# The first pair of a fused attention and cosine-gated MLP: order of gate and conversion, weight sums on VectorE, two homes for temporaries, exponentials in two steps

## Chip, cores and metric

The kernel runs on one core of one Trainium2 chip. The metric is the device time of one execution in microseconds (us). All arithmetic is in 32-bit floats; the two weight matrices arrive as 64-bit floats.

## What is computed

```python
# x: (8, 8, 512, 64)   state: (8, 8, 32, 64)   w_in: (512, 2048)   w_out: (2048, 512)
scores = scale * x @ state.T;  a  = softmax(scores);   xread = a @ state      # per batch and head
scores2 = scale * state @ x.T; a2 = softmax(scores2);  sread = a2 @ x
y = concatenate([xread, sread], axis=2)          # (8, 8, 544, 64)
y = y.transpose(0, 2, 1, 3).reshape(8 * 544, 512)
h = y @ w_in
g = h * cos(h)
out = g @ w_out
```

## The kernel before

**Tiles and steps.** The work goes by batches (eight), two of which make a pair, and in each batch by 16 tiles of 128 rows of `h`. One tile is one step, so the first pair is steps 0 to 31. For a tile PE (TensorE) makes 128 x 512 of `h` in PSUM (`hidden`, L490), and the gate follows in four instructions: ScalarE rounds `h` to an integer (`gate`, L560), VectorE (DVE) subtracts (`gate2`, L563), ScalarE takes the sine (`gate3`, L566), DVE multiplies (`gate4`, L580) and so puts `g` into `g_all`. In steps 0 to 27 (`first_pair`) a tile has one of two PSUM buffers, which the product frees.

**The order is written out by hand.** The program has no scheduler: the order of the instructions in the source is the order on each engine, and each engine runs its own in order. `plan(b)` lists for each step what else is done for attention: on PE, on ScalarE (`x_act`, `y_act`, `z_act`) and on DVE (`x_dve`, between the gate's subtraction and product; `y_dve`, behind the product). Its parts are the token turns (L310), the scores (L328), `max1`, `shift` and `exp1` for the first softmax, `max2` and `exp2` for the second, `sums`, `inverse`, `spread1`, `norm1`. Exponential and sine lie in different activation tables, so that a change from one to the other brings an ACT_TABLE_LOAD.

**Conversion.** The weights come in 18 loads of up to 1 MB of raw 64-bit numbers into three buffers (quads 9 to 11 of `g_all`; a quad is four slots of 128 x 512). `conv_at` gives a step to each of loads 4 to 17: in that step ScalarE makes two passes over it (L243, L246), in the next step DVE two (L249, L252) and Pool (GpSimd) the last addition (L257). As soon as DVE has read a raw buffer, SP issues the next load (`fetch`, L212). SP also issues, in its own order, token loads and x_b loads (L131), stores of weight blocks (L673), loads of weight blocks into a ring of four (L683), and the output's stores (L622).

**Two forms of the second product.** In steps 4 to 27 PE multiplies two quarters of `w_out` directly (`first_product`, `second_product`, L633). From step 29 on it works by the seven-product scheme of Strassen and Winograd on two levels: seven products with combinations of the quarters A11, A12, A21, A22, and each of these again in seven stages (L745) with combinations of its own four blocks. Pool forms the sums of `g` that the stages need (L692), and sums of the weights of the hidden tiles (`sw_sums`, L523).

**The weights of the seven-product scheme** are prepared once, in steps 16 to 25 (A12's in step 50). `weight_sum` combines whole quarters in place (`SQ` = A21 + A22, A21' = A11 - A21, A22' = SQ - A11, SQ' = A12 - A22'; L1092). `inner_weights(which, m)` makes, for one matrix, four temporaries t1 to t4 of 128 x 512 on Pool (L671) in one fixed quad (`TEMPS`, quad 4), and has SP store eight blocks in device memory (`blocks_kept`): four of the matrix, four temporaries. The next `inner_weights` writes the same quad, so it waits until the stores have read it. `weights_at[step]` holds these calls; they come behind the tile's own code in a step. Before the change, in this order: 16 A22; 17 SQ on Pool; 18 SQ, and A21' on DVE; 19 A11; 20 A22' on Pool; 21 A21'; 22 A22'; 24 SQ' on DVE; 25 SQ'. "Last set" below is that of SQ'.

**Order of a conversion step**, cut to what the change moves:

```python
gate(t); gate2(t)
go(1); go(3)                 # x_act, x_dve
convert(last, "bcdf")        # L249, L252 on DVE, L257 on Pool, next raw load
if conv >= 0 and not todo[1]: convert(conv, "1")
gate3(t)
gate4(t)
```

Of the kernel before, what the change touches and what calls it, by code (L numbers as in the profile page):

```python
# [13 lines left out]
ALU = mybir.AluOpType  # L14
# [8 lines left out]
def kernel(  # L23
# [8 lines left out]
    nc = tc.nc  # L32
# [43 lines left out]
    def quad(n):  # L76
        return g_all[:, QT * n:QT * n + QT]
# [186 lines left out]
    class Attention:  # L264
# [115 lines left out]
            self.exp2()  # L380

        def inverse(self, v):
            w = v.rearrange("p (a b) -> p b a", b=2)
            nc.vector.tensor_scalar(w, w, 1e-9, None, op0=ALU.add)
            nc.vector.reciprocal(v, v)
# [273 lines left out]
        m = m.rearrange("p (k i) (m d) -> p m k i d", k=2, m=2)  # L659
        return m[:, 0, 0], m[:, 0, 1], m[:, 1, 0], m[:, 1, 1]  # L660

    def inner_weights(which, m, temps=TEMPS):

        m11, m12, m21, m22 = quarters(m)
        t1, t2, t3, t4 = [quad(temps)[:, n].rearrange("p (i d) -> p i d", d=P)
                          for n in range(4)]
        for o, x1, x2, op in ((t1, m21, m22, ALU.add),
                              (t2, t1, m11, ALU.subtract),
                              (t3, m11, m21, ALU.subtract),
                              (t4, m12, t2, ALU.subtract)):  # L670
            nc.gpsimd.tensor_tensor(o, x1, x2, op=op)  # L671
        for n, block in enumerate((m11, m12, t4, m22, t1, t2, t3, m21)):
            nc.sync.dma_start(  # L673
                out=blocks_kept[which, n].rearrange("p (i d) -> p i d", d=P),
                in_=block)

    stage_list = []

# [279 lines left out]
    def plan(b):  # L958
        pe, x_act, y_act, x_dve, y_dve, z_act = [
            {s: [] for s in range(NF)} for _ in range(6)]  # L960

        def prod(s, b, nt, *bank):
            pe[s].append((b, "products", nt) + bank)
            x_act[s].append((b, "products_kept", nt) + bank)

        def pairs(s, b, name, kept, i):
            pe[s] += [(b, name, i), (b, name, i + 1)]
            x_act[s].append((b, kept, i))
            y_act[s].append((b, kept, i + 1))

        def early(b, s):
            if b == 1:
                pairs(s[0], b, "tokens", "tokens_kept", 0)
                pairs(s[1], b, "tokens", "tokens_kept", 2)
            else:
                for k in range(NK):
                    to = (x_dve, y_dve)[k % 2]
                    to[s[k // 2]].append((b, "tokens_turned", k))
            pe[s[2]].append((b, "scores"))
            x_dve[s[2]].append((b, "max1"))  # L980
            x_dve[s[3]].append((b, "spread1"))
            y_dve[s[3]].append((b, "shift"))
            if b == 1:
                x_dve[s[4]].append((b, "max2"))
                y_act[s[4]].append((b, "exps"))
            else:
                y_dve[s[4] - 1].append((b, "max2"))
                z_act[s[4]].append((b, "exps"))
            if b == 1:
                x_dve[s[5]].append((b, "sums"))  # L990
                y_dve[s[5]].append((b, "spread1"))
                x_dve[s[6]].append((b, "norm1"))
            else:
                y_dve[s[4]].append((b, "sums1"))
                x_dve[s[5]].append((b, "spread2"))
                y_dve[s[5]].append((b, "norm1"))

        def late(b, s):
            pairs(s[0], b, "turn", "turn_kept", 0)
            pe[s[1]].append((b, "reads", 0))  # L1000
            pe[s[2]].append((b, "reads", 1))
            x_dve[s[2]].append((b, "keep"))
            if len(s) > 3:
                turned(b, s[3])

        def turned(b, s):
            pe[s].append((b, "keep2"))
            x_act[s].append((b, "keep3"))


        if b == 0:
            pe[0].append((0, "products", 0, SIDE, HC, WC))
            y_dve[0] += [(0, "products_taken", 0, SIDE, HC, WC),
                         (0, "inverse2")]
            prod(7, 0, 2, SIDE)
            prod(11, 0, 3)
            prod(13, 1, 0, SIDE)
            late(0, (1, 2, 3, 4))
            early(1, (5, 6, 7, 8, 9, 10, 11))
            late(1, (12, 13, 14))  # L1020
        else:
            bank = (SIDE,) if b == 1 else ()
            if b == 1:
                turned(1, 0)
            prod(0, b, 1, *bank)
            prod(3, b, 2, *bank)
            prod(8, b, 3, *bank)
            if b + 1 < B:
                prod(12, b + 1, 0)
                early(b + 1, (1 + (b == 1), 2 + (b == 1), 4, 5, 7, 8, 9))  # L1030
                late(b + 1, (9, 10, 11, 15))
        return pe, x_act, y_act, x_dve, y_dve, z_act
# [37 lines left out]
    for n in range(B // 2):  # L1070
        end = n == B // 2 - 1
        for r, engine, o, x1, x2, half in (
                ((25, 26), dve, 0, 2, 0, 0), ((27, 28), dve, 0, 2, 0, 1),
                ((31, 31), pool, 2, 3, 2, 0), ((33, 33), dve, 0, 3, 0, 0),
                ((34, 34 + (not end)), dve, 0, 3, 0, 1),
                ((35, 36), dve, 2, 3, 2, 1),
                ((38 - end,) * 2, pool, 1, 1, 0, 0),
                ((39 - end,) * 2, pool, 1, 1, 0, 1)):
            for i in range(2):
                outer_at[PERIOD * n + r[i]].append(  # L1080
                    (engine, n, o, x1, x2, half, i))
# [3 lines left out]
                     for r in (o, x1, x2)]  # L1085
        sub(engine, o, x1, x2)

    def weight_sum(engine, o, x1, x2, op):
        n = 1 if engine is pool else 2
        for i in range(0, QT, n):  # L1090
            o_, x1_, x2_ = [quad(q)[:, i:i + n] for q in (o, x1, x2)]
            engine.tensor_tensor(o_, x1_, x2_, op=op)  # L1092

    def last_weights():
        temps = quads_free.pop(0)
        inner_weights(1, a12, temps)
        weights_at[53].append(lambda: quads_free.extend([A12, temps]))

    A11, A12, A21, A22, SQ = 5, 6, 7, 8, 11
    add_, sub_ = ALU.add, ALU.subtract  # L1100
    for at_, what in (
            (15, lambda: quads_free.append(10)),
            (16, lambda: inner_weights(2, a22)),
            (17, lambda: quads_free.append(9)),
            (17, lambda: weight_sum(pool, SQ, A21, A22, add_)),
            (18, lambda: inner_weights(3, matrix(SQ))),
            (18, lambda: weight_sum(dve, A21, A11, A21, sub_)),
            (19, lambda: inner_weights(0, a11)),
            (20, lambda: weight_sum(pool, A22, SQ, A11, sub_)),
            (21, lambda: inner_weights(5, matrix(A21))),  # L1110
            (22, lambda: inner_weights(4, matrix(A22))),
            (23, lambda: quads_free.append(A11)),
            (24, lambda: weight_sum(dve, SQ, A12, A22, sub_)),
            (25, lambda: quads_free.append(A21)),
            (25, lambda: inner_weights(6, matrix(SQ))),
            (27, lambda: quads_free.extend([A22, SQ, TEMPS])),
            (50, last_weights)):
        weights_at[at_].append(what)

# [19 lines left out]
    def first_pair(step, t):  # L1139
        last, conv = conv_at.get(step - 1, -1), conv_at.get(step, -1)  # L1140
        if step == 4:
            warm(1, acc[0])
        if step != 1:
            hidden(t)
        if step == 0:
            hidden(all_tiles[1])
            warm(3, acc[0])
            gate(t)
            gate2(t)
            convert(3, "bcdf")  # L1150
            convert(4, "1")
            go(0)
        else:
            go(0)
            if step == 5:
                states(1, side_banks[0])
            gate(t)
            gate2(t)
            if step == 3:
                warm(4, acc[0])  # L1160
                part(0, "products", 1, SIDE)
            go(1)
            go(3)
            if step == 1:
                convert(4, "bcdf")
            elif last >= 0:
                convert(last, "bcdf")
            if conv >= 0 and not todo[1]:
                convert(conv, "1")
        gate3(t)  # L1170
        go(5)
        if step == 3:
            part(0, "products_kept", 1, SIDE)
        gate4(t)
        if conv >= 0 and todo[1] and step > 0:
            convert(conv, "1")
        if step == 6:
            states_kept(1, side_banks[0])
        go(2)
        if conv >= 0:  # L1180
            convert(conv, "2")
        go(4)
# [124 lines left out]
```

## Time and profile before

| | us |
|---|---|
| median of 4 runs | 765.42 (764.69 to 765.94) |
| profiled execution | 765.93 |
| its span, first to last instruction | 764.1 |
| busy in the span: PE / DVE / ScalarE / Pool | 720.5 / 490.4 / 330.9 / 517.5 |

The profile comes from one execution. Its page gives busy time by engine, the span in 40 equal slices (each digit the busy share in tenths), and the chain of work that ended last: a walk back from the last instruction, at each step to what released it. Asked for a stretch, the trace gives that chain in order of time (start, length, what), or a timeline by engine: start, length, engine, line, operation, operands, count, and in brackets the engine's idle time just before and what ended it. A name like L692 is a line of the kernel before. In the kernel after the change the same code stands one to some thirty lines further down. SPq is SP's queue of DMA issues. PEclk, the clock granted to PE, was 0.991 of full speed over the span.

### The profile page before, as it was taken

Reading aid. Unit: us, or ns where it says so; the run is one execution under the profiler, and the core shown is the slowest. Engines: PE = TensorE matmul, PEld = TensorE weight load, DVE = VectorE, ACT = ScalarE, POOL = GpSimd, SP = SyncE. Lnnn points to the kernel's source line nnn. Section 1 sums busy time; section 2 is a strip of 40 time slices with the busy share of each in tenths; the row PEclk is TensorE's granted clock in tenths of the full one; section 3 lists DMA queues with packets and bytes.
Section 4 is the critical chain, followed back from the end, with each engine's and each line's share of the span. In section 5 each row is a group of like instructions: output and inputs, shape, how many; then the busy total and the mean of one; then the engine's idle time right before and its main releaser. Section 6 shows DMA issues by size and latency. Waiting matters only on the chain.

```text
span 764.1 us, 10471 instructions
## 1 busy us (share of the span) xinstructions
PE 720.5 (94%) x3552; PEld 506.6 (66%) x3552; DVE 490.4 (64%) x683; ACT 330.9 (43%) x538; POOL 517.5 (68%) x480
## 2 busy tenths in 40 slices
PE   8988887779999999999999999999999999999998
PEld 3443322336777876677768876677778767888886
DVE  5768786783876656685966666759746446264650
ACT  3877962633454445434373445343634432211110
POOL 2344267779699895368998953489989534799600
PEclk9999998999999999999999999999999999999999
DMA  8495359779423685476225943682224556445661
GB/s 247 166 275 167 125 121 267 224 246 182 116 87 80 138 236 142 109 146 166 73 80 111 183 112 95 134 195 84 71 69 124 111 155 163 114 147 184 185 156 41
DMA packets 210356, 111.32 MB, mean 146 GB/s; under 512 B 158272, under 2 KB 173120, under 8 KB 210304
## 3 DMA queue, kind: packets, MB, share of 16 engines
q1 hardware_dynamic: 209216, 110.14, 55.5%
q8 instruction: 28, 0.46, 0.2%
q10 hardware_dynamic: 960, 0.39, 0.2%
q14 instruction: 24, 0.20, 0.1%
q0 software_dynamic: 128, 0.13, 0.1%
HBM read 87.03 MB, written 23.59 MB: 145 GB/s over the span
## 4 chain that ended last, share of the span: by engine, by line
PE 60%; POOL 20%; DVE 5%; DMA 4%; issue 4%; ACT 3%; SPq 3%; POOLq 0%; DVEq 0%; ACTq 0%
PE o L745 31%; POOL g_all L692 12%; PE h L490 10%; PE h L540 9%; POOL g_all L671 4%; PE at L328 3%; PE at L846 2%; POOL swS_all L523 2%; PE at L425 1%; DMA blocks_kept<-g_all 1%; DMA g_all<-blocks_kept 1%; DMA x_b<-in_x_dram 1%; POOL sw L523 1%; SPq L131 1%; SPq L673 1%
## 5 line engine op out<-in xcount | busy, mean ns | idle before, releaser
L692 POOL TENSOR_TENSOR g_all<-g_all 128x512 f32<-128x512 f32 x256 | 336.7, 1350 | 108.3 <-PE o L745 62.9
L745 PE MATMUL o<-g_all 128*128 128x256 f32 x1456 | 345.2, 382 | 4.8 <-POOL g_all L692 3.4
L745 PEld LDWEIGHTS o<-g_all 128*128 128x128 f32 x1456 | 273.9, 191 | 65.7 <-issue 18.0
L563 DVE TENSOR_TENSOR q_all<-q_all,h 128x1024 f32<-128x1024 int32 (+1 forms) x88 | 85.4, 970 | 59.6 <-ACT q_all L560 59.5
L490 PE MATMUL h<-aT,sw 128*128 128x512 f32 x224 | 109.0, 611 | 12.7 <-DVE g_all L580 12.0
L566 ACT ACTIVATE q_all<-q_all,halfpi 128x1024 f32<-128x1024 f32 (+1 forms) x88 | 84.2, 957 | 61.7 <-DVE q_all L563 61.6
L580 DVE TENSOR_TENSOR g_all<-h,q_all 128x1024 f32<-128x1024 f32 (+1 forms) x88 | 85.7, 974 | 34.5 <-ACT q_all L566 32.2
L560 ACT ACTIVATE q_all<-h 128x1024 int32<-128x1024 f32 (+1 forms) x88 | 73.3, 833 | 75.4 <-DVE g_all L580 32.3
L490 PEld LDWEIGHTS h<-aT,sw 128*128 128x128 f32 x224 | 41.7, 194 | 59.8 <-issue 32.2
L549 DVE TENSOR_TENSOR h<-h,sums_all 128x256 f32<-128x256 f32 x72 | 30.9, 429 | 63.7 <-PE h L540 49.0
L692 DVE TENSOR_TENSOR g_all<-g_all 128x1024 f32<-128x1024 f32 x40 | 56.9, 1437 | 0.1
L540 PE MATMUL h<-aS_all,swS_all 128*128 128x256 f32 x144 | 45.8, 400 | 7.5 <-POOL swS_all L523 5.7
L540 PE MATMUL h<-aT,sw 128*128 128x256 f32 x144 | 44.6, 392 | 3.0 <-DVE g_all L580 2.5
L750 ACT COPY o<-o 128x256 f32<-128x256 f32 x26 | 9.3, 357 | 88.1 <-PE o L745 88.1
L671 POOL TENSOR_TENSOR g_all<-g_all 128x512 f32<-128x512 f32 x28 | 37.8, 1370 | 12.5 <-DMA blocks_kept<-g_all 11.9
L257 POOL TENSOR_TENSOR w_in<-w_in,aS_all 128x1024 int32<-128x1024 int32 (+1 forms) x10 | 19.3, 1926 | 37.4 <-DVE w_in L252 20.3
L540 PE MATMUL h<-aS_all,sw 128*128 128x256 f32 x144 | 43.6, 384 | 0.0
L540 PEld LDWEIGHTS h<-aS_all,swS_all 128*128 128x128 f32 x144 | 25.5, 191 | 26.8 <-POOL g_all L692 7.5
L756 ACT COPY o<-sums_all 128x256 f32<-128x256 f32 x26 | 9.8, 377 | 74.0 <-PE o L745 74.0
L603 DVE SCALAR_TENSOR_TENSOR held<-o,held 128x512 f32<-128x512 f32 x40 | 27.1, 680 | 21.3 <-PE o L745 20.8
L461 ACT COPY sw<-at 128x512 f32<-128x512 f32 x50 | 26.8, 588 | 31.3 <-PE at L328 31.3
L257 POOL TENSOR_TENSOR g_all<-g_all,aS_all 128x1024 int32<-128x1024 int32 x8 | 18.9, 2368 | 29.9 <-DVE g_all L252 22.6
(112 smaller groups left out, 867.5 us busy)
## 6 DMA issues: line engine op xcount, KB each, us to landing
g_all<-blocks_kept SPq DMA_DIRECT2D x202, 256.0 KB, 2.8
blocks_kept<-g_all SPq DMA_DIRECT2D x56, 256.0 KB, 3.0
g_all<-in_moe_w_out_dram SPq DMA_DIRECT2D x8, 1024.0 KB, 5.0
out_dram<-ot SPq DMA_DIRECT2D x128, 64.0 KB, 2.0
g_all<-in_moe_w_in_dram SPq DMA_DIRECT2D x6, 1024.0 KB, 5.7
xT<-in_x_dram SPq DMA_DIRECT2D x96, 64.0 KB, 3.0
x_b<-in_x_dram SPq DMA_DIRECT2D x24, 256.0 KB, 4.9
x_b<-in_x_dram SPq DMA_DIRECT2D x16, 128.0 KB, 4.0
```

Of the source, the lines that this page charges most:

```text
L257: nc.gpsimd.tensor_tensor(bits, bits, e, op=ALU.add)
L490: nc.tensor.matmul(out=t.hp, lhsT=t.lhs(i), rhs=t.rhs(i), start=(i == 0), stop=(i == t.kn - 1))
L540: nc.tensor.matmul(out=out_, lhsT=w, rhs=r, start=start, stop=True, skip_group_check=True)
L549: nc.vector.tensor_tensor(o, h2[:, LO], sums_all[:, 0], op=ALU.add)
L560: nc.scalar.activation(t.q.bitcast(I32), t.hp, func=ACTF.Copy, bias=0.25)
L563: nc.vector.tensor_tensor(t.q, t.q.bitcast(I32), t.hp, op=ALU.subtract)
L566: nc.scalar.activation(t.q, t.q, func=ACTF.Sin, bias=halfpi, scale=-TWO_PI)
L580: nc.vector.tensor_tensor(g, t.hp, t.q, op=ALU.mult)
L603: nc.vector.scalar_tensor_tensor(out=out.t[:, ch], in0=bank, scalar=TWO_PI, in1=b.t[:, ch], op0=ALU.mult, op1=ALU.add)
L671: nc.gpsimd.tensor_tensor(o, x1, x2, op=op)
L692: engine.tensor_tensor(o[:, i:i + n], x1[:, i:i + n], x2[:, i:i + n], op=ALU.subtract)
L745: nc.tensor.matmul(out=o, lhsT=ring[(self.first + k) % NB][:, i], rhs=g[:, i], start=(start and i == 0), stop=(i == QT - 1), skip_group_ch ...
```

## The change

1. In the first pair's steps the gate's product goes ahead of DVE's and Pool's conversion of the last load. (Step 0 stays as it was.)
2. All four weight sums run on DVE, each in two pieces of 128 x 1024, a piece a step: SQ in 16 and 17, A21' in 18 and 19, A22' in 20 and 22, SQ' in 23 and 25. None is left on Pool.
3. Pool's temporaries have two homes: quad 4 and `aS_all`, which conversion uses until step 16 and the hidden tiles from step 28. They take turns. A11's set comes first, one temporary in each of steps 12 to 15, and Pool's instructions are 128 x 256 in place of 128 x 512. The sets come in steps 12 to 15, 17, 19, 21, 23, 26.
4. The stores of a set are handed to SP at the start of the following step.
5. For batch 2 the second softmax's maximum and the first's exponential are in step 22, its sums and the second exponential in step 23, the inverse and `spread1` in step 24, `norm1` in step 25; before, the two exponentials were together in step 23. ScalarE's first copy of the turned second softmax follows the sine of its step.
6. One DVE sum of `g` (L692) moves from step 25 to 24.

```diff
-    def inner_weights(which, m, temps=TEMPS):
+    def inner_weights(which, m, temps, pieces=range(4), n=2):
...
-            nc.gpsimd.tensor_tensor(o, x1, x2, op=op)
-        for n, block in enumerate((m11, m12, t4, m22, t1, t2, t3, m21)):
-            nc.sync.dma_start(
...
+            for j in range(0, QT, n):
+                nc.gpsimd.tensor_tensor(o[:, j:j + n], x1[:, j:j + n],
+                                        x2[:, j:j + n], op=op)
+
+        def send():
+            for n, block in enumerate((m11, m12, t4, m22, t1, t2, t3, m21)):
+                nc.sync.dma_start(
...
+        if 3 in pieces:
+            stores_due.append(send)
...
+            elif b == 2:
+                x_dve[s[4] - 1].append((b, "max2"))
+                z_act[s[4] - 1].append((b, "exp1"))
+                x_dve[s[4]].append((b, "sums1"))
+                z_act[s[4]].append((b, "exp2"))
+                x_dve[s[5]].append((b, "inverse", None))
+                y_dve[s[5]].append((b, "spread1"))
+                x_dve[s[5] + 1].append((b, "norm1"))
...
+            if b == 2:
+                x_act[s[0]].remove((b, "turn_kept", 0))
+                y_act[s[0]].insert(0, (b, "turn_kept", 0))
...
-                ((25, 26), dve, 0, 2, 0, 0), ((27, 28), dve, 0, 2, 0, 1),
+                ((25 - (not n), 26), dve, 0, 2, 0, 0),
+                ((27, 28), dve, 0, 2, 0, 1), ((31, 31), pool, 2, 3, 2, 0), ((33, 33), dve, 0, 3, 0, 0),
...
+    def weight_sum(o, x1, x2, op, i):
+        o_, x1_, x2_ = [quad(q)[:, 2 * i:2 * i + 2] for q in (o, x1, x2)]
+        nc.vector.tensor_tensor(o_, x1_, x2_, op=op)
...
+    temps = [quad(TEMPS), aS_all.rearrange("p n i s -> p (n i s)").rearrange(
+        "p (t s) -> p t s", s=S)]
+    for i in range(QT):
+        weights_at[12 + i].append(lambda i=i: inner_weights(
+            0, a11, temps[0], (i,)))
+    for steps, o, x1, x2, op in (
+            ((16, 17), SQ, A21, A22, ALU.add),
+            ((18, 19), A21, A11, A21, ALU.subtract),
+            ((20, 22), A22, SQ, A11, ALU.subtract),
+            ((23, 25), SQ, A12, A22, ALU.subtract)):
+        for i in range(2):
+            weights_at[steps[i]].append(
+                lambda o=o, x1=x1, x2=x2, op=op, i=i: weight_sum(
+                    o, x1, x2, op, i))
     for at_, what in (
             (15, lambda: quads_free.append(10)),
-            (16, lambda: inner_weights(2, a22)),
             (17, lambda: quads_free.append(9)),
-            (17, lambda: weight_sum(pool, SQ, A21, A22, add_)),
-            (18, lambda: inner_weights(3, matrix(SQ))),
-            (18, lambda: weight_sum(dve, A21, A11, A21, sub_)),
-            (19, lambda: inner_weights(0, a11)),
-            (20, lambda: weight_sum(pool, A22, SQ, A11, sub_)),
-            (21, lambda: inner_weights(5, matrix(A21))),
-            (22, lambda: inner_weights(4, matrix(A22))),
+            (17, lambda: inner_weights(2, a22, temps[0])),
+            (19, lambda: inner_weights(3, matrix(SQ), temps[1])),
+            (21, lambda: inner_weights(5, matrix(A21), temps[0])),
+            (23, lambda: inner_weights(4, matrix(A22), temps[1])),
             (23, lambda: quads_free.append(A11)),
-            (24, lambda: weight_sum(dve, SQ, A12, A22, sub_)),
             (25, lambda: quads_free.append(A21)),
-            (25, lambda: inner_weights(6, matrix(SQ))),
-            (27, lambda: quads_free.extend([A22, SQ, TEMPS])),
+            (26, lambda: inner_weights(6, matrix(SQ), temps[0])),
+            (27, lambda: quads_free.append(A22)),
+            (28, lambda: quads_free.extend([SQ, TEMPS])),
...
             go(1)
             go(3)
-            if step == 1:
-                convert(4, "bcdf")
-            elif last >= 0:
-                convert(last, "bcdf")
             if conv >= 0 and not todo[1]:
                 convert(conv, "1")
         gate3(t)
...
         gate4(t)
+        if last >= 0:
+            convert(last, "bcdf")
```

More of the change, by code (lines that the diff above doesn't have):

```diff
@@ L382, in inverse @@
         def inverse(self, v):
+            v = self.i12 if v is None else v
             w = v.rearrange("p (a b) -> p b a", b=2)
@@ L660, in quarters @@
         return m[:, 0, 0], m[:, 0, 1], m[:, 1, 0], m[:, 1, 1]
-    def inner_weights(which, m, temps=TEMPS):
+    def inner_weights(which, m, temps, pieces=range(4), n=2):
         m11, m12, m21, m22 = quarters(m)
-        t1, t2, t3, t4 = [quad(temps)[:, n].rearrange("p (i d) -> p i d", d=P)
+        t1, t2, t3, t4 = [temps[:, n].rearrange("p (i d) -> p i d", d=P)
                           for n in range(4)]
[L667 to L671, printed above, removed]
-        for n, block in enumerate((m11, m12, t4, m22, t1, t2, t3, m21)):
-            nc.sync.dma_start(
-                out=blocks_kept[which, n].rearrange("p (i d) -> p i d", d=P),
-                in_=block)
+        for i in pieces:
+            o, x1, x2, op = ((t1, m21, m22, ALU.add),
+                             (t2, t1, m11, ALU.subtract),
+                             (t3, m11, m21, ALU.subtract),
+                             (t4, m12, t2, ALU.subtract))[i]
+            for j in range(0, QT, n):
[4 more added lines that the diff above has]
+                nc.sync.dma_start(
+                    out=blocks_kept[which, n].rearrange("p (i d) -> p i d",
+                                                        d=P),
+                    in_=block)
+        if 3 in pieces:
+            stores_due.append(send)
     stage_list = []
@@ L992, in early @@
                 x_dve[s[6]].append((b, "norm1"))
-            else:
+            elif b > 2:
                 y_dve[s[4]].append((b, "sums1"))
@@ L1072 @@
         for r, engine, o, x1, x2, half in (
-                ((25, 26), dve, 0, 2, 0, 0), ((27, 28), dve, 0, 2, 0, 1),
-                ((31, 31), pool, 2, 3, 2, 0), ((33, 33), dve, 0, 3, 0, 0),
+                ((25 - (not n), 26), dve, 0, 2, 0, 0),
+                ((27, 28), dve, 0, 2, 0, 1), ((31, 31), pool, 2, 3, 2, 0), ((33, 33), dve, 0, 3, 0, 0),
                 ((34, 34 + (not end)), dve, 0, 3, 0, 1),
@@ L1086, in outer_sum @@
         sub(engine, o, x1, x2)
[L1088 to L1092, printed above, removed]
+    def weight_sum(o, x1, x2, op, i):
+        o_, x1_, x2_ = [quad(q)[:, 2 * i:2 * i + 2] for q in (o, x1, x2)]
+        nc.vector.tensor_tensor(o_, x1_, x2_, op=op)
     def last_weights():
         temps = quads_free.pop(0)
-        inner_weights(1, a12, temps)
+        inner_weights(1, a12, quad(temps), n=QT)
@@ L1097, in last_weights @@
         weights_at[53].append(lambda: quads_free.extend([A12, temps]))
     A11, A12, A21, A22, SQ = 5, 6, 7, 8, 11
-    add_, sub_ = ALU.add, ALU.subtract
+    temps = [quad(TEMPS), aS_all.rearrange("p n i s -> p (n i s)").rearrange(
[12 more added lines that the diff above has]
+                    o, x1, x2, op, i))
```

## Prediction, made before the result

> **What bounds the kernel now.** I read the page's slices first, then the chain that ended last, in order of time, then the timelines of VectorE (DVE), ScalarE and GpSimd (Pool) where that chain leaves TensorE.
>
> ```profile
> PE   8988887779999999999999999999999999999998
> POOL 2344267779699895368998953489989534799600
> ```
>
> A slice is 19.1 us. PE has holes only in the first nine, which is the first pair (to about 172 us). After that PE is the bound, apart from three Pool stretches that come once in each later pair and that the change doesn't touch. So the change can win or lose only ahead of the point where PE is full, and later work moves with that point. The chain there, in order of time:
>
> ```profile
> 107.00 2.36 POOL g_all L257
> ...
> 114.41 3.81 POOL g_all L1092 x4
> 118.22 2.10 issue
> 120.35 2.31 POOL g_all L671
> 122.74 3.73 POOL g_all L671 x3
> ...
> 127.94 2.72 DMA blocks_kept<-g_all
> ...
> 137.47 2.82 DMA blocks_kept<-g_all
> ...
> 156.58 2.74 DMA blocks_kept<-g_all
> ...
> 181.61 3.06 DMA g_all<-blocks_kept
> ```
>
> From the last conversion (L257) to 165 us the chain is Pool: weight sums (L1092), temporaries (L671), and between two sets of temporaries the wait until the last set is stored. From there SP issues without a hole until the block that PE takes at 184.8. The timelines show the two costs:
>
> ```profile
> 116.88 2.27 DVE L1092 TENSOR_TENSOR g_all<-g_all 128x1024 f32<-128x1024 f32 x1 [3.88 <-POOL g_all L1092]
> 120.30 1.22 DVE L1092 TENSOR_TENSOR g_all<-g_all 128x1024 f32<-128x1024 f32 x1 [1.16 <-POOL g_all L1092]
> 122.16 0.72 ACT L566 ACTIVATE q_all<-q_all,halfpi 128x512 f32<-128x512 f32 x1 [8.39 <-DVE q_all L563]
> 130.74 5.09 POOL L671 TENSOR_TENSOR g_all<-g_all 128x512 f32<-128x512 f32 x4 [4.28 <-DMA blocks_kept<-g_all]
> 159.45 5.76 POOL L671 TENSOR_TENSOR g_all<-g_all 128x512 f32<-128x512 f32 x4 [3.83 <-DMA blocks_kept<-g_all]
> 108.83 0.69 DVE L580 TENSOR_TENSOR g_all<-h,q_all 128x512 f32<-128x512 f32 x1 [0.79 <-ACT q_all L566]
> 139.08 1.06 ACT L366 ACTIVATE aT<-aT 128x1024 f32<-128x1024 f32 x1
> ```
>
> DVE's sum of step 18 waits for Pool's sum of step 17, and the gates behind it wait with it: no sine for 8.39 us. Pool waits about four microseconds for stores (4.28, 3.77, 3.83). The 0.79 is what DVE idles when nothing stands between the gate's subtraction (L563) and its product (L580).
>
> **The sum, by step.** I follow the start of L563 of each step, before against after, and then Pool's last set of temporaries, which ended at 165.21.
>
> *Gate product ahead of conversion, steps 1 to 9 and 12 to 16.* The conversion's L249 and L252 (0.69 and 1.23) stood in the shadow of the sine; now DVE idles 0.79 first, and L252 ends 0.79 + 0.68 = 1.5 later in its step. It costs nothing where the next step's L563 waited longer than 0.79 for ScalarE anyway (after steps 1, 4 and 5: 1.44, 1.08 and 3.54 us). It costs in three places:
> - Steps 2 to 6. SP issues the next raw load only behind L252, and such a load lands 5.0 to 5.7 us later (median rows). In step 2 the delay is 1.5; in step 3 the load that was issued at 32.58 comes 1.5 later, ScalarE's first conversion (it waited 0.2 for it already) holds up the sine, and L252 ends 2.5 later. Queued behind it on SP are the eight x_b loads at 42.06 which PE waited for (6.18 us in the chain). So step 6 starts at 57.7, not 55.28.
> - Step 6. The states' copy (L171) now stands behind L249 and L252: another 0.9 for the scores of batch 1 that PE makes from it. Step 9 starts at 74.3, not 70.82: 3.5 late. Steps 9 to 13 keep that.
> - Steps 14 and 15. The last two raw loads are issued behind L252 of steps 12 and 13; the last one made ScalarE wait 0.74 before. With 1.5 more, the first conversion, which in these two steps stands ahead of the sine, holds up the gate by about 0.8 each. Step 16 starts at 108.05, not 103.06: 5.0 late.
>
> From below this is 0 (all of it covered by ScalarE, which is nearly full there); from above 14 x 0.79 = 11.1 if DVE ends last in every conversion step.
>
> *Temporaries of A11 in steps 12 to 15.* Eight Pool instructions of 256 elements. There is no such row; 128 elements take 0.46 (L523) and 512 take 1.27 (L671), so between 0.64 (half) and 1.27, and I take 0.73 on the line between them. They stand in Pool's holes of 1.95 to 2.94 us between conversions: nothing, and if that cover is gone 1.5 a step.
>
> *Weight sums on DVE.* Eight of 1.22 (L1092 undisturbed; 2.27 is the disturbed one). The first, in step 16, adds 1.2: step 17 starts at 113.6, not 107.37, 6.2 late. Then each step is the sum of its DVE issues (0.60 for L563 and L580 each when followed closely, 0.6 to 0.7 for a token turn, 1.2 for maximum, spread or shift, 0.79 or 0.17 idle) and 1.15 for the sum, with 0.4 for disturbance by Pool (it was 1.05 and 0.0 in the two L1092 rows above, with Pool pieces of 1.27; I take 0.5 of the one and scale it to 0.73 pieces, rounded up): step 17 takes 3.6 (it waits for Pool's last conversion), 18 to 20 4.3 each, 21 3.8: 20.3. Before, these steps took 133.08 - 107.37 = 25.7, since the wait for Pool was in them. Step 22 starts at 133.9, not 133.08: 0.8 late.
>
> The Trainium skill, "SBUF — State Buffer", section "Who interferes with whom", speaks against this part: a DVE instruction with two SBUF inputs and a GpSimd instruction that reads SBUF lock each other out for a whole instruction. By that rule each of the five sums ahead of step 22 could wait one full piece, and my estimate of the Pool piece would make it 1.7 us more than I take. The 2.27 row agrees; the 1.22 row, beside a Pool set that took 6.11 instead of 5.10, shows that the wait can also fall on Pool.
>
> *Exponentials in two steps (22 and 23).* Two more table loads, 1.28 each by the ACT_TABLE_LOAD rows. ScalarE after the sine of step 22: load, exp1 1.06, gate copy 0.6, load, sine 0.72, load, two exponentials 1.4, gate copy, two copies 1.06, load, sine: the product of step 24 comes 11.4 after that sine, against 10.8 before. But DVE's sums, which stood behind the product before (L1092 twice, 2.35), now fill its waits in steps 22 and 23, and norm1 of step 25 hides a sine. Step 26 starts 19.3 after step 22 (20.1 before): 153.2, as before (153.18).
>
> "ScalarE: Activation LUTs", section "What ACT_TABLE_LOAD costs", gives 1283 ns and a drain of about 1380 ns behind it. The row at 139.08 starts right at the end of its load (137.79 and 1.28), so this trace has no such drain; by the page's figure the two loads would be an estimated 2.8 us dearer.
>
> *Pool's chain.* With two homes, no set waits for the set just ahead of it to be stored: a set is stored within 3.5 us of SP issue and 3.0 of landing, and its home is written again about two sets (13 us) later. SP keeps its order of loads and stores; stores are handed over one step later, but SP waited for Pool there anyway (28.2 us in SP's waits on L671). Pool runs A22, SQ and A21 from about 116 to 137, A22' from 137 and the last set right behind DVE's last sum at 153.2: 8 x 0.73 and 0.7 of disturbance, end at 159.9. Before, it ended at 165.21. **Difference: 5.3 us earlier.**
>
> *What is late next.* Behind that end stand SP's last stores (3.5 us) and its train of token loads, output stores and blocks, and Pool's row sums and L523, for which PE idled 4.9 us at 171.9. All of these follow Pool's end as before. The DVE start of step 28 is about level (161.1, 161.38), but step 28 took 7.6 us before, because Pool's late work disturbed DVE (1.48 and 1.37 for L509, which takes 0.43 and 0.67 undisturbed); it should take about 5.5, so DVE doesn't take over. PE would be ready for its block at about 176 and gets it at 179.4, not 184.7: the block, through SP, still ends last, and 5.3 is kept. From there the order is the same to the end.
>
> The profiled execution took 765.93 (span 764.1); less 5.3 that is 760.6. The median of the runs is 0.5 lower: **760.1**.
>
> **Rivals.**
> - *The gates' delay is wholly covered.* ScalarE is busy 16.34 of 21 us in steps 12 to 16, which speaks for it; the SP order behind L252 against it. No 5.0 late: 755.1.
> - *No change.* DVE ends last in nearly every conversion step: 13 x 0.79 = 10.3 instead of 5.0. For it: DVE is busy 17.63 of 21 us in the same stretch. Against: L563 waits for ScalarE in most earlier steps. About 765.4.
> - *Slower: raw loads pace the first pair.* Each load is issued 1.5 later and must land within two steps. If most landings are near the row's longest (6.5) rather than its median (5.0), each conversion step pays the 1.5 in full; above seven of fourteen steps (10.3) the change loses. Ten steps are 15: 15 - 10.3 = 4.7 slower, 770.1. For it: ScalarE already waited for loads at 37.9 and 98.4. Against: only 0.2 and 0.74 us.
>
> **How the numbers follow.** The forecast 0.58, covered delay 0.12, no change 0.12, slower 0.18. About 0.2% (1.5 us) is what a measurement of this kernel can tell from no change. Part of the no-change case falls outside it: faster 0.70, same 0.10, slower 0.20. The range goes from the covered case, 755.0, to 767.0, which takes in no change and the mild end of the slower case.
>
> **What would show it.** Right: the 8.39 wait gone; L1092 on DVE alone, eight or so at 1.2 to 1.6; Pool's waits for blocks_kept under 2 us in all; the last set of temporaries ending near 160; step 9 about 3.5 late and step 16 about 5; four table loads near 135 to 146. Wrong: step 16 more than 8 late, ScalarE waiting for moe_w DMAs by more than a microsecond at a time, or Pool's end early by 5 while PE's block comes no earlier.

## Result and the profile after

The kernel after the change took 767.91 us in the median (39 runs, 765.98 to 769.16), the kernel before 765.43 in the same sessions (58 runs): a ratio of 1.0029 with an interval of 1.0024 to 1.0035. So it is slower by 2.2 us, and the forecast was 760.1. The profiled execution took 768.88 (span 767.1), 2.95 more than that of before.

From the page after the change, busy tenths in the 40 slices:

```profile
PE   8989867888999999999999999999999999999998
POOL 2343289569699896367998953489989535799610
```

PE still has its holes in the first nine slices and is full behind them, so here too the first pair decides most. The train of steps, followed as in the prediction by the start of DVE's subtraction (L563 before, L564 after):

| us | before | predicted | after |
|---|---|---|---|
| step 6 | 55.28 | 57.7 | 57.22 |
| step 9 | 70.82 | 74.3 | 73.64 |
| step 16 | 103.06 | 108.05 | 108.54 |
| step 17 | 107.37 | 113.6 | 114.91 |
| step 22 | 133.08 | 133.9 | 137.27 |
| step 26 | 153.18 | 153.2 | 156.32 |
| Pool's last set ends | 165.21 | 159.9 | 162.95 |
| step 28 | 161.38 | 161.1 | 166.38 |
| step 32 | 187.15 | 181.85 (187.15 - 5.3) | 189.38 |

Pool's last set did come earlier, by 2.3 us, and yet the end came later. Behind step 32 the distance to before stays at 2.23 until step 35 and grows to 3.0 by step 56, which was not followed up. GpSimd's timeline after the change (start, length, engine, line; in brackets the idle time ahead and what ended it) shows that Pool is no longer what is late:

```profile
156.44 6.51 POOL L674 TENSOR_TENSOR g_all<-g_all 128x256 f32<-128x256 f32 x8 [8.99 <-DVE g_all L1110]
...
170.46 1.31 POOL L701 TENSOR_TENSOR g_all<-g_all 128x512 f32<-128x512 f32 x1 [2.83 <-DVE g_all L701]
```

It waits 8.99 us for DVE's last weight sum, and later 2.83 for a sum of `g`, both of which stand in the train of steps. The chain that ended last, in order of time, in the stretch where it was Pool, SP and the weight blocks before:

```profile
168.29 0.03 SPq L131
...
172.17 1.89 DMA out_dram<-ot
174.06 0.69 DVE ot L614
174.75 2.02 DVE aS_all L510 x2
176.76 0.61 DVE q_all L564
...
177.40 0.72 ACT q_all L567
178.12 0.27 ACT o L759
178.39 0.31 ACT sums_all L760
...
178.74 2.70 PE o L754 x8
181.44 2.70 PE h L491 x4
```

No weight block ends last any more. Up to 174.06 the walk goes through SP's token loads and the landing of an output store. That store held nothing up: in DVE's timeline L614 starts at 174.05 with no idle time ahead of it, and in the kernel of experiment 7, where the walk stays on DVE, the step takes the same 4.72 us. PE waits for DVE and ScalarE in step 30 (2.98 us), and then works on its own.

### The profile page after: what moved, and what is told of

Same layout as the page of the kernel before. It is cut to its first block, busy times and chain, and to the rows that moved or that the text cites. A ratio compares the mean times of both kernels' runs of the same rounds, so it can differ in the third digit from the quotient of the medians.

```text
span 767.1 us, 10498 instructions
## 1 busy us (share of the span) xinstructions
PE 723.4 (94%) x3552; PEld 508.2 (66%) x3552; DVE 494.3 (64%) x687; ACT 333.2 (43%) x540; POOL 516.9 (67%) x496
## 4 chain that ended last, share of the span: by engine, by line
PE 54%; POOL 18%; issue 2%; DVE 2%; ACT 1%; DMA 1%; SPq 0%; POOLq 0%; DVEq 0%
PE o L754 29%; POOL g_all L701 14%; PE h L491 9%; PE h L541 8%; POOL swS_all L524 2%; PE at L855 2%; PE at L328 2%; POOL sw L524 1%; PE at L426 1%; PE o L855 1%; DMA g_all<-blocks_kept 1%; DVE g_all L701 1%; SPq L131 0%; ACT q_all L567 0%; DVE xT L310 0%
## 5 line engine op out<-in xcount | busy, mean ns | idle before, releaser
L701 POOL TENSOR_TENSOR g_all<-g_all 128x512 f32<-128x512 f32 x256 | 336.5, 1347 | 112.3 <-PE o L754 63.6
L491 PE MATMUL h<-aT,sw 128*128 128x512 f32 x224 | 112.9, 629 | 15.8 <-DVE g_all L581 15.3
L564 DVE TENSOR_TENSOR q_all<-q_all,h 128x1024 f32<-128x1024 int32 (+1 forms) x88 | 85.3, 970 | 55.8 <-ACT q_all L561 55.6
L701 DVE TENSOR_TENSOR g_all<-g_all 128x1024 f32<-128x1024 f32 x40 | 55.7, 1409 | 0.1
L257 POOL TENSOR_TENSOR w_in<-w_in,aS_all 128x1024 int32<-128x1024 int32 (+1 forms) x10 | 19.3, 1928 | 41.1 <-DVE w_in L252 19.4
L674 POOL TENSOR_TENSOR g_all<-g_all 128x256 f32<-128x256 f32 (+1 forms) x36 | 34.5, 991 | 9.6 <-DVE g_all L1110 9.0
L604 DVE SCALAR_TENSOR_TENSOR held<-o,held 128x512 f32<-128x512 f32 x40 | 27.1, 680 | 21.3 <-PE o L754 20.8
```

The lines of the kernel that those rows point to most:

```text
L257: nc.gpsimd.tensor_tensor(bits, bits, e, op=ALU.add)
L491: nc.tensor.matmul(out=t.hp, lhsT=t.lhs(i), rhs=t.rhs(i), start=(i == 0), stop=(i == t.kn - 1))
L564: nc.vector.tensor_tensor(t.q, t.q.bitcast(I32), t.hp, op=ALU.subtract)
L604: nc.vector.scalar_tensor_tensor(out=out.t[:, ch], in0=bank, scalar=TWO_PI, in1=b.t[:, ch], op0=ALU.mult, op1=ALU.add)
L674: nc.gpsimd.tensor_tensor(o[:, j:j + n], x1[:, j:j + n], x2[:, j:j + n], op=op)
L701: engine.tensor_tensor(o[:, i:i + n], x1[:, i:i + n], x2[:, i:i + n], op=ALU.subtract)
```

## Experiments

Every kernel was compared with the kernel before in the same session, and what two kernels differ by is taken from their ratios; "the train" is the start of the subtraction in a step, from one profiled execution each. Between executions of one kernel the time varies by 2 to 5 us, so the medians carry the verdicts, and the trains show where a cost lies. The trains also differ where nothing was edited: step 0 starts at 25.12 us before, at 25.80 after, and at 25.12 to 26.53 in the kernels below.

**1. The kernel after with conversion ahead of the gate's product, as before the change**

```diff
             go(1)
             go(3)
+            if last >= 0:
+                convert(last, "bcdf")
...
         gate4(t)
-        if last >= 0:
-            convert(last, "bcdf")
```

> The changed kernel with conversion ahead of the gate's product again, as before; all else stays changed. Theory (the train of steps ends last after the change, and the order of gate and conversion made it late): step 16 starts near 104.5 instead of 108.5 (103.1 before the change), step 28 near 162.5 instead of 166.4, and the time is 763.5 to 764.5, faster than before the change. Rival (Pool's early temporaries and the first sum on DVE make the conversion steps late, not the order): step 16 stays above 106.5 and the time above 766.5.

763.04 us (761.75 to 765.71), ratio 0.9973 (0.9961 to 0.9986). Step 16 starts at 103.98 instead of 108.54, step 28 at 159.87 instead of 166.38. Undone, this part alone turns the loss into a gain: 0.56% between the two ratios, 4.3 us. Still, the gain over before is 2.1 us and not the 10.3 that the prediction left if the gates weren't delayed.

**2. The same part alone: the kernel before with the gate's product first**

```diff
-            if step == 1:
-                convert(4, "bcdf")
-            elif last >= 0:
-                convert(last, "bcdf")
...
         gate4(t)
+        if last >= 0:
+            convert(last, "bcdf")
```

> The kernel before with nothing changed but the gate's product ahead of conversion. Theory: step 16 starts 3.5 to 4.5 late (107) with no temporaries of Pool in the way, Pool's chain behind the last conversion moves with it, and the time is 768.5 to 770. Rival (the order is covered by ScalarE, the delay comes from Pool's pieces): step 16 less than 1.5 late, time within 1 of 765.4.

769.93 us (768.48 to 771.34), ratio 1.006 (1.0042 to 1.0077): 4.6 us slower. Step 16 starts at 106.59, 3.5 late (0.4 of it is there at step 0), where nothing else of the change is present. Both ways round the order costs about the same.

**3. The kernel after with A22' one step later**

```diff
-            ((20, 22), A22, SQ, A11, ALU.subtract),
+            ((21, 22), A22, SQ, A11, ALU.subtract),
```

> The changed kernel with the first piece of A22' a step later (21 and 22 instead of 20 and 22). Theory (in step 20 DVE waits 2.8 for the last store of A22's blocks, which landed at 131.97, and the whole train waits with it): that wait is gone, step 22 starts at 134.5 to 135.5 instead of 137.3, and the time is 765 to 766.5. Rival (the wait stands in slack that the exponentials or PE take up later): step 28 within 1 of 166.4 and the time 767.5 to 768.

766.38 us (763.14 to 767.94), ratio 1.001 (0.9996 to 1.0023). What it takes away is this wait on DVE's timeline after the change, in step 20:

```profile
128.58 0.65 DVE L581 TENSOR_TENSOR g_all<-h,q_all 128x512 f32<-128x512 f32 x1
132.05 1.77 DVE L1110 TENSOR_TENSOR g_all<-g_all 128x1024 f32<-128x1024 f32 x1 [2.82 <-POOL g_all L674]
133.74 0.67 DVE L564 TENSOR_TENSOR q_all<-q_all,h 128x512 f32<-128x512 int32 x1
```

Pool's A22 set, which is named, had ended at 124.84, so something behind it was awaited. SP's queue after the change, asked for in pieces, shows what:

```profile
117.36 4.35 SPq L131 DMA_DIRECT2D x_b<-in_x_dram  x4
121.76 1.91 SPq L679 DMA_DIRECT2D blocks_kept<-g_all  x2
...
124.87 4.09 SPq L679 DMA_DIRECT2D blocks_kept<-g_all  x6
```

These are the eight stores of A22's set in the order of the source: two of A22's own blocks (m11, m12), then the temporary t4, for which SP waits until Pool's set has ended (124.84), then m22, t1, t2 and t3, and last A22's block m21. That one was issued at 127.58 and landed at 131.97. A22' overwrites A22 in place, and m21 lies in the half that the first piece writes, so this piece can't begin ahead of that. The four x_b loads ahead of these stores don't decide it, since SP waits 1.1 us for Pool behind them; what holds up m21 is its place at the end, behind the temporaries (another order was not tried). With the piece in step 21 the wait is gone and step 22 starts at 133.47 instead of 137.27. The time gained 1.5 us in the medians; the profiled execution (763.14, the fastest of twelve) shows more than the others had.

**4. The kernel after with batch 2's exponentials together again**

```diff
-                x_dve[s[4] - 1].append((b, "max2"))
-                z_act[s[4] - 1].append((b, "exp1"))
-                x_dve[s[4]].append((b, "sums1"))
-                z_act[s[4]].append((b, "exp2"))
...
```

> The changed kernel with batch 2's exponentials together in step 23 again (two table loads fewer). Theory (the steps 22 to 26 took 19.1 against 20.1 before, so the split pays): step 26 starts up to 1 later and the time is 767.5 to 769. Rival (the two more loads, 2.6 in all, are what makes the train late): step 26 2 or more earlier, time 765.5 or less.

767.18 us (765.89 to 769.72), ratio 1.0026 (1.0012 to 1.0039): the interval takes in that of the kernel after. The split is worth nothing that these runs can tell. ScalarE's timeline after the change has the four loads, at 138.71, 141.56, 143.69 and 147.90, each 1.28 us, and the next activation starts at the load's end. The train agrees: from step 22 to 26 it takes 19.5 us here and 19.05 with the split.

**5. The kernel after with A11's temporaries in steps 8 to 11**

```diff
-        weights_at[12 + i].append(lambda i=i: inner_weights(
+        weights_at[8 + i].append(lambda i=i: inner_weights(
```

> The kernel after with A11's four temporaries in steps 8 to 11 (no conversion goes on there, and Pool had a hole of 11 to 12 us) instead of 12 to 15. Theory (Pool's A11 pieces slow the conversion's two DVE instructions beside them, 0.4 us each, eight of them): L249 and L252 back to 0.68 and 1.23 in steps 13 to 16, step 16 starts 1 to 2 us earlier (107.0 instead of 108.54), step 22 about 136, and the time 0.5 to 1.5 lower (766.5 to 767.5). Rival (the pieces lie in cover, the steps are paced by something else): step 16 within 0.4 of 108.54, time unchanged.

765.71 us (763.36 to 767.36), ratio 1.0006 (0.9995 to 1.0016), about 1.8 us less than after. DVE's timeline in step 15, first after, then in this kernel:

```profile
105.78 1.16 DVE L249 TENSOR_SCALAR g_all<-g_all 128x1024 int32<-128x1024 int32 x1
106.98 1.63 DVE L252 SCALAR_TENSOR_TENSOR g_all<-g_all 128x1024 int32<-128x1024 int32 x1
```

```profile
105.14 0.68 DVE L249 TENSOR_SCALAR g_all<-g_all 128x1024 int32<-128x1024 int32 x1
105.86 1.22 DVE L252 SCALAR_TENSOR_TENSOR g_all<-g_all 128x1024 int32<-128x1024 int32 x1
```

Pool's two pieces of A11 in a step cost DVE's two conversion instructions up to 0.5 each; without them steps 9 to 16 take 33.7 us instead of 34.9 (the other 0.3 by which step 16 is earlier is there at step 9 already). The holes that Pool had there were not free for DVE.

**6. The kernel after with one home for the temporaries**

```diff
-    temps = [quad(TEMPS), aS_all.rearrange("p n i s -> p (n i s)").rearrange(
-        "p (t s) -> p t s", s=S)]
+    temps = [quad(TEMPS), quad(TEMPS)]
```

> The kernel after with one home for Pool's temporaries (quad 4 for all sets) instead of two. Theory (the second home is what took the waits for stores off Pool, 11.9 us in three waits before): Pool waits 3 to 4 us ahead of three sets or more, its last set ends 3 or more later than 162.95, and the time is 1 to 4 us longer (769 to 772). Rival (the sets are paced by DVE's sums and are a whole step apart, so the stores have landed anyway): no wait above 1 us, last set within 1 of 162.95, time within 1 of 767.9.

772.18 us (770.89 to 772.58), ratio 1.0091 (1.0078 to 1.0105): 4.7 us more than after. GpSimd's timeline:

```profile
129.44 6.53 POOL L674 TENSOR_TENSOR g_all<-g_all 128x256 f32<-128x256 f32 x8 [4.91 <-DMA blocks_kept<-g_all]
139.80 6.53 POOL L674 TENSOR_TENSOR g_all<-g_all 128x256 f32<-128x256 f32 x8 [3.83 <-DVE g_all L1110]
150.16 9.58 POOL L674 TENSOR_TENSOR g_all<-g_all 128x256 f32<-128x256 f32 x8 [3.83 <-DMA blocks_kept<-g_all]
163.56 6.70 POOL L674 TENSOR_TENSOR g_all<-g_all 128x256 f32<-128x256 f32 x8 [3.83 <-DVE g_all L701]
```

The waits for stores are back, and in four sets. Two of them are put down to DVE, but in these too the store of t1, whose place a set writes first, landed just ahead of the set's start (at 139.67 and 163.43). The last set ends at 170.3 instead of 162.95, and Pool is again what is late behind step 28 (steps 28 to 32 take 27.3 us against 23.0). The second home does what the prediction gave it.

**7. Two repairs together: conversion first, and A22' in 21 and 22.** The edits are those of 1 and 3.

> The kernel after with both repairs: conversion ahead of the gate's product as before the change, and the two pieces of A22' in steps 21 and 22. Theory (the two costs add up, since both stand in the same train of steps): step 16 near 104, step 22 near 129 (132.66 with the first repair alone, less 3.5), step 28 near 156, time 760 to 762 against 763.0 with the first repair alone. Rival (from step 28 on another chain is late: Pool's last set, its stores and the blocks behind them, or PE itself): step 28 earlier by 3, but step 33 and the time as with the first repair alone, 763.

759.30 us (758.69 to 761.29), ratio 0.9932 (0.9918 to 0.9946): 5.2 us faster than before and the fastest of all. Step 16 starts at 103.73, step 22 at 128.90, step 28 at 156.11, step 32 at 179.43. Together the two repairs are worth 7.4 us, against 4.3 and 1.5 one at a time, which the intervals allow: the two costs add up, and no other chain takes over.

**8. The kernel of 7 with SQ and A22' summed on Pool**

```diff
-            ((16, 17), SQ, A21, A22, ALU.add),
...
-            ((21, 22), A22, SQ, A11, ALU.subtract),
...
+            (17, lambda: pool_sum(SQ, A21, A22, ALU.add)),
...
+            (20, lambda: pool_sum(A22, SQ, A11, ALU.subtract)),
```

> The same kernel as that with two repairs, but SQ and A22' summed on Pool in four pieces of 128 x 512 (steps 17 and 20) as before the change; A21' and SQ' stay on DVE. Theory (the sums on DVE took the 8.39 us wait out of step 18): Pool's sum of SQ begins behind its last conversion and A22's set, near 120, DVE's sum of A21' in step 18 waits for it by 5 us or more, step 22 near 134 instead of 128.9, time 763 to 766. Rival (DVE is the train's bound, and 4 x 1.2 taken off it pays for the wait): step 22 within 1.5 of 128.9 and time within 1.5 of 759.3.

767.49 us (766.85 to 768.51), ratio 1.0029 (1.0018 to 1.004): 7.4 us slower than 7, more than expected. Two rows of DVE's timeline, and GpSimd's beside the second:

```profile
120.80 2.27 DVE L1110 TENSOR_TENSOR g_all<-g_all 128x1024 f32<-128x1024 f32 x1 [6.31 <-POOL g_all L1115]
...
140.62 6.98 DVE L1110 TENSOR_TENSOR g_all<-g_all 128x1024 f32<-128x1024 f32 x1
```

```profile
141.02 1.39 POOL L674 TENSOR_TENSOR aS_all<-g_all 128x256 f32<-128x256 f32 x2
142.38 1.40 POOL L674 TENSOR_TENSOR aS_all<-aS_all,g_all 128x256 f32<-128x256 f32 x2
143.75 1.40 POOL L674 TENSOR_TENSOR aS_all<-g_all 128x256 f32<-128x256 f32 x2
145.12 1.39 POOL L674 TENSOR_TENSOR aS_all<-g_all,aS_all 128x256 f32<-128x256 f32 x2
```

The wait for Pool's sum is back (6.31), and step 22 is 4.8 late, as expected. The rest was not foreseen: a sum that takes 1.2 on its own stood for 6.98 and ended 1.1 us after Pool's set did, and steps 26 to 28 take 10.06 us instead of 8.15.

**9. The kernel of 7 with Pool's temporaries in pieces of 512**

```diff
-    def inner_weights(which, m, temps, pieces=range(4), n=2):
+    def inner_weights(which, m, temps, pieces=range(4), n=4):
```

> The kernel after with conversion ahead of the product and the pieces of A22' in 21 and 22, and Pool's temporaries in instructions of 128 x 512 instead of 128 x 256. Theory (a DVE sum and a Pool instruction hold each other up for a piece at a time): the sums L1110 beside a set take up to 2.3 instead of up to 1.6, L249 and L252 beside A11's pieces 1.9 or more, a set takes 5.1 undisturbed instead of 5.7; the train is 1 to 3 us later at step 28 and the time 760 to 762. Rival (the piece's size does not matter to DVE; fewer Pool instructions are cheaper): sets 0.6 shorter, step 28 as before (156.1), time 759.

763.91 us (761.76 to 765.26), ratio 0.998 (0.9969 to 0.9991): 3.7 us slower than 7 by the ratios. The sums beside a set took 1.56 to 2.05 and the conversion's L252 2.17 to 2.19 instead of 1.63: small pieces on Pool are worth having. Not all of the 3.7 is their size, though: one sum took 3.04. It began behind Pool's conversion and ended 1.08 after that, so it stood for the whole of it; in 7 the same sum came ahead of it and took 1.21:

```profile
109.16 2.34 POOL L257 TENSOR_TENSOR g_all<-g_all,aS_all 128x1024 int32<-128x1024 int32 x1 [1.23 <-DVE g_all L252]
109.54 3.04 DVE L1110 TENSOR_TENSOR g_all<-g_all 128x1024 f32<-128x1024 f32 x1
```

In the first kernel of 10, with pieces of 256, this sum came behind Pool's conversion too and took 3.05.

**10. The kernel of 7 with more of it rearranged.** The first moves A11's temporaries to steps 8 to 11 as in 5; the second joins the exponentials too, as in 4.

> The kernel after with conversion ahead of the product, the pieces of A22' in 21 and 22, and A11's temporaries in steps 8 to 11. It stands between the run with the first two (759.3) and the run that also joined the exponentials (761.4). If splitting the exponentials is worth something once the waits before it are gone: step 24 about 1.3 us earlier than 140.68, step 28 near 156, time 759 to 760. If moving A11's temporaries is what cost: step 28 near 157, time 761 to 762.

> The kernel after with conversion ahead of the product, the pieces of A22' in 21 and 22, A11's temporaries in steps 8 to 11, and batch 2's two exponentials together in step 23 as before the change. If the costs add up: step 16 near 103, step 22 near 128, step 28 near 155; the exponentials are worth under 1 us either way (they were, alone). Time 759 to 762. If Pool's end or PE's own work is the bound by then: 762 to 764.

760.81 us (759.01 to 763.74), ratio 0.9942 (0.9925 to 0.9958), and 761.36 (759.54 to 762.68), ratio 0.995 (0.9935 to 0.9964): neither is better than 7, and their intervals overlap with its own. In the first, steps 9 to 16 take 32.85 us instead of 33.64, and step 16 takes 7.28 instead of 6.25, so what the move saves is spent again in the next step, by the sum of 3.05 that experiment 9 mentions. (Its train is 1.3 late at step 0 already, which is not the edit.) So nothing is left here of the 1.8 us of experiment 5.

## Why the prediction was wrong

**The gates' delay was right in kind; its size was partly luck.** Step 6 was 0.5, step 9 0.7 earlier than predicted, and step 16 0.5 later, but 0.7 of the delay is there at step 0, ahead of the change. Counted from step 0 the order alone is 3.15 late at step 16, not 5.0 (experiment 2), and A11's temporaries add 1.2 (experiment 5), which the prediction had at nothing, in Pool's holes. Its other end, 1.5 a step if the cover is gone, was too much: two pieces cost about 0.9 of DVE's time in a step, of which 0.3 reached the train.

**The step that failed is "What is late next".** It had the weight block, through SP, end last, so that Pool's 5.3 us came through, and the train of steps about level at step 28. The runs show the train ending last, 5.0 late at step 28. From the predicted step 32 to the measured one, 181.85 to 189.38, are 7.5 us; differences of the table's rows give:
- 1.3 at step 17: 0.5 at step 16, and 0.8 in that step, where L252 and the first sum took 1.63 and 1.74 us beside Pool and the prediction counted 1.2 for each.
- 2.1 from step 17 to 22, 22.36 instead of 20.3. "4.3 each" for a step was dear: without the wait in step 20 the stretch takes 18.9 (experiment 3). The wait was missed because the prediction followed the stores of a set only as the readers of the temporaries' home. The same eight stores read the matrix's own four blocks, which the next weight sum overwrites.
- -0.2 from 22 to 26: 19.05 instead of 19.3. The two extra table loads were priced right; no drain is behind them.
- 2.2 from 26 to 28: 10.06 instead of 7.9. In the kernels of 1, 3, 5 and 7 it takes 8.15. Of the 1.9 between, 1.2 lie in step 26: its four matmuls took 3.31 us instead of 1.98, behind the same hole of 2.68, and ScalarE waited for them. The rest is DVE's sum L701 in step 27, 2.10 beside Pool's sums against 1.39 in experiment 1. Whether the slow matmuls belong to the change or only to the profiled execution, which took 1.0 more than the median, stays open.
- 2.3 from 28 to 32. The prediction let these steps shrink with Pool's end, from 25.8 to 20.7. Step 28 did, to 5.6 as it said; the three behind it did not shrink as far. The four take 23.0 here and 23.3 in the kernels of 1 and 7, though Pool's last set ends anywhere from 155.6 to 163.0. In PE's timeline there is the same hole in step 30, with the same matmuls behind it. First after, then in the kernels of 7, 9 and 4:

```profile
178.74 2.70 PE L754 MATMUL o<-g_all 128*128 128x256 f32 x8 [2.98 <-ACT sums_all L760]
```

```profile
168.79 2.72 PE L754 MATMUL o<-g_all 128*128 128x256 f32 x8 [2.98 <-ACT sums_all L760]
```

```profile
173.65 2.00 PE L754 MATMUL o<-g_all 128*128 128x256 f32 x8 [2.97 <-ACT sums_all L760]
```

```profile
178.56 3.78 PE L754 MATMUL o<-g_all 128*128 128x256 f32 x8 [2.97 <-ACT sums_all L760]
```

Behind the same hole these eight matmuls take 2.70, 2.72, 2.00 and 3.78 us, and with that the four steps take 21.3 in the kernel of 9 and 24.7 in that of 4. So even the fastest of these trains needs more than 20.7, and by most of the profiles the train had only some 2.5 us of slack to Pool before (25.8 - 23.2). A Pool that ends earlier gains that much and no more unless the train comes earlier too, and here the train came 5.0 late at step 28. "About level" was the decisive number, and it wasn't derived as carefully as Pool's.

**What was right:** the 8.39 wait is gone; L1110 took 1.18 to 1.79 on DVE (1.2 to 1.6 predicted); Pool's last set came earlier, though at 162.95 and not at 159.9 (a sum whose own terms, 153.2, 8 x 0.73 and 0.7, make 159.7); two homes take the waits for stores off Pool (0.58 us is left, ahead of A22's set, which uses the same home as A11's; the homes alternate only from there on). The sums on DVE pay, as experiment 8 shows. The mechanism works where the train is let go: the kernel of 7 reaches 759.3.

**The rivals.** None fits. "Raw loads pace the first pair" has the sign, but its point, seven steps that pay 1.5 in full, was not reached: step 16 is 5.5 late and not over 10. One of the signs that were to show the prediction wrong did come, once: ScalarE waited 1.15 us for the last raw load, where it waited 0.74 before. "PE gets its block no earlier" isn't what happened either: the block was no longer awaited.

**On the lock between DVE and Pool.** The rows are 1.18 to 1.79 us for a sum beside pieces of 256 (0.73 each), 1.56 to 2.05 beside pieces of 512 (1.27 each), 3.04 behind Pool's conversion (2.34), and 6.98 once beside eight pieces of 256. The prediction's 1.55 was near the mark: the five sums ahead of step 22 took 1.54 in the mean. The Trainium skill, "SBUF — State Buffer", section "Who interferes with whom", has the one that comes second blocked until the first finishes. All of these rows fit, since a sum lost no more than one Pool instruction, but the last, which stood for eight.

## What to carry to other kernels

When an engine off the path is made faster, work out how much slack the next chain has by measuring what that chain takes in a stretch where it waits for nothing; the gain ends there. Ask of each store not only which scratch buffer it frees but what else it reads that is overwritten in place, and what it stands behind in its queue. And a change of six parts is best taken apart: here two parts were sound (4.7 us for the second home, 7.4 for the sums of SQ and A22' on DVE), one was worth nothing that could be told, and three misplaced ones spent it all (the order of gate and conversion 4.3, A11's temporaries in steps 12 to 15 1.8, the first piece of A22' 1.5). These prices were taken in different kernels and don't add up exactly; the later handing over of the stores and the moved sum of `g` weren't tried alone.

## What the runs showed of the hardware

**Holes and the granted clock.** In PE's timeline after the change the same four matmuls take twice as long behind some holes:

```profile
117.12 3.78 PE L491 MATMUL h<-aT,sw 128*128 128x512 f32 x4 [4.39 <-DVE g_all L581]
124.14 1.88 PE L491 MATMUL h<-aT,sw 128*128 128x512 f32 x4
...
136.20 3.78 PE L491 MATMUL h<-aT,sw 128*128 128x512 f32 x4 [3.82 <-DVE g_all L581]
```

In the kernel of 7 the holes of these steps are 1.2 to 1.6 us, the matmuls take 1.98, and the granted clock is 1.00 from 110 to 170 us, where after it is 0.75 to 0.91 from 110 to 160. So a late DVE also makes PE slower for a while. The Trainium skill, "TensorE: Matmul & The Clock Gate", section "What's actually happening", has half speed after an idle window of about 3.4 us; the two holes of 4.39 and 3.82 agree. But the 3.31 of step 26 followed a hole of 2.68, and in experiment 1 a hole of 2.68 at the same place was followed by 1.98; and behind the hole of 2.97 or 2.98 in step 30 the same eight matmuls took 2.00, 2.70 and 3.78. So shorter holes can cost as well, and the last hole's length alone doesn't decide. In steps 28 to 32 the profiles of 4 and 9 differ by 3.4 us, 3.1 of it in these eight matmuls and the four behind them.

**A sum that stood for a whole set.** Why the DVE sum of experiment 8 stood through eight Pool instructions (6.98 us), while others beside an equal set lost 0.6 at most, stays open.
